# Two-layer attention and MLP block on one core: the first chunk's residual is added from the bf16 input in place, with the list of priorities annealed again

## The chip, the cores and the metric

The kernel runs on one core of a Trainium2 chip. The metric is the device time of one execution in microseconds. Times of before are of five runs; a profiled execution of the same kernel has its own time and its own span (from its first to its last instruction). In the profile PE is TensorE, PEld its weight loads, DVE VectorE, ACT ScalarE, POOL GpSimd and SP SyncE, which here only issues DMAs.

## The reference

The input x has 2048 rows of 576 numbers in bf16. Two layers are applied, each made of an attention block and an MLP block, both with a residual, and with the same weights in both layers:

```python
def _A_ref(x, wqkv, wo):          # H = 32 heads of Dh = 18, window W = 256
    q, k, v = split(x @ wqkv)
    scores = q k^T * Dh**-0.5, masked to 0 <= i - j < W
    return (softmax(scores) v) @ wo

def _B_ref(x, w1, b1, w2, b2):    # F = 4608
    y = _layernorm(x)
    return gelu(y @ w1 + b1) @ w2 + b2

x = x + _A_ref(_layernorm(x), A_wqkv, A_wo)
x = x + _B_ref(_layernorm(x), B_w1, B_b1, B_w2, B_b2)
(the same two lines again)
```

(`split` and the masked line are shortened here; the rest is as it stands.)

## The kernel before

The rows are cut into 16 tiles of 128, four tiles to a chunk, so that there are eight chunks: 0 to 3 of the first layer, 4 to 7 of the second. For each chunk k the kernel does: normalise and project to q, k, v (`qkv`, matmuls on L671, copies by DVE on L710 and L697); attention in eight groups of four heads (`E`: scores on L757, exp by ACT on L766, mask by POOL on L787, product with v on L804, division by the sums on L814 and L819 into `attq`); `tail`: transposes of `attq` to `attT` by DMA (L848), the output projection with `wo` (L671 again), the residual add (`resid`, L838, by DVE), statistics (L592, L594), the reciprocal root (L603, L605, by POOL), the normalised tile (L615, L620) and its transpose by DMA to `xnTm` (L635); and the MLP in two halves of 2304 hidden columns: `G_part` (matmuls on L881 and L893, gelu by ACT on L896 into `hT`) and `mm2` (matmuls on L922, and the residual add through `resid` again).

The residual stream lives in `x_res`, float32, all 16 tiles. Two things share memory with other data. The bf16 input `x_in` lies in the memory of `hT`, which is first written by the gelus of chunk 0; these writes wait for the readers of the input tiles under them (`xin_under`, L898). The q and k of chunk 1 (`qx`, `kx`) lie in the part of `x_res` that belongs to chunks 3 and 2; that is why scores of chunk 1 are shown as `ps<-x_res`. Input tiles get into `x_res` by four DMAs of four tiles each that widen bf16 to float32, issued by POOL (`x_load`, L555 to L558, shown on L536 where all plain DMAs are recorded). For chunk 0:

```python
wo_load()                             # on ACT's queue, after attq of group 0
x_load(0, n0, ["aq1"], -4)            # after attq of group 1
x_load(CH[1][1], CH[1][2], ["aq3"], 0)
w1_load(-1, ["aq3"])
```

SP issues, in one order, the DMA transposes (of q and k on L729, of normalised tiles on L635, of `attq` on L848) and the loads of w1 and w2. ACT issues the loads of wqkv and of wo. SP, ACT and POOL each issue in their instruction order, so a DMA whose wait is not yet met holds all that is behind it.

The order of every engine's instructions is made when the kernel is built. Each operation is entered with the engine, what it reads and writes, a cost, a latency and a priority, and `Plan.schedule` (L257) lays the operations out as a list scheduler: of those that are ready it takes the one that can start first, and of equal ones the one with the smaller priority number; matmul filler goes into the first free of three PSUM banks. `PL.nudge` (L446 to L451) adds a number to the priority of named stages: "q2.1" is the projection of tile 1 of chunk 2, "ea2" and "eb2" the attention of chunk 2, "t2" its tail, "ga2" and "gb2" the halves of its MLP's first matmul, "ma2" and "mb2" of its second, "ld0+" the loads entered with chunk 0. With other numbers the same operations come in another order. Where PE would be idle early in the run, the planner puts in matmuls on a tile of zeros (L579), which nothing reads.

Of the kernel before, what the change touches and what calls it, by code (L numbers as in the profile page):

```python
# [8 lines left out]
ALU = mybir.AluOpType  # L9
# [31 lines left out]
class Sched:  # L41
# [23 lines left out]
    def add(self, eng, fn, reads=(), writes=(), dma=None, ring=4):  # L65
        waits = {}

        def want(ev):
            c, v, _e = ev
            if waits.get(c, 0) < v:  # L70
                waits[c] = v

        for r in reads:
            lw = self.last_write.get(r)
            if lw is not None and not (eng == "pe" and lw[2] == "pe"):
                want(lw)
        for w in writes:
            for rd in self.readers.get(w, ()):
                if rd[2] != eng or rd[3]:
                    want(rd[:3])  # L80
            lw = self.last_write.get(w)
            if lw is not None and not (eng == "pe" and lw[2] == "pe"):
                want(lw)
        if dma is None:
            assert eng != "sp"
            c = self.cnt[eng]
            amount = 1
        else:
            rg = self.ring(eng, dma, ring)
            c = rg.sems[rg.i % rg.k]  # L90
            rg.i += 1
            amount = 16
            if c.val > 0:
                want((c, c.val, None))
        wl = []
        wd = self.waited[eng]
        for cc, v in waits.items():
            if wd.get(cc, 0) >= v:
                continue
            wd[cc] = v  # L100
            wl.append((cc, v))
        c.val += amount
        own = None if dma is not None else eng
        ev = (c, c.val, own)
        self.steps[eng].append(Step(eng, fn, wl, c, amount))
        for w in writes:
            self.last_write[w] = ev
            self.readers[w] = []
        for r in reads:
            self.readers.setdefault(r, []).append((c, c.val, own, dma is not None))  # L110
        return ev
# [297 lines left out]
def build_kernel(nc, A_x, A_wqkv, A_wo, B_x, B_w1, B_b1, B_w2, B_b2, out):  # L409
# [12 lines left out]
    HB = 288  # L422
# [19 lines left out]
    PL = Plan(S, 7)  # L442
    add = PL.add


    PL.nudge = {"b": 1.83, "ea0": -1.98, "ld0+": 40.46, "eb0": 2.23, "q1.0": -6.02, "q1.1": 1.09, "t0": 6.35, "ga0": -26.49, "q2.0": 12.46,  # L446
                "q2.2": 12.06, "q2.3": 21.72, "t1": -35.56, "ea2": -3.78, "ga1": -4.7, "ma1": 15.69, "ma1+": -9.39, "q3.2": -1.65, "q3.3": -7.2,
                "eb3": 1.74, "ma2": 3.52, "q4.0": 39.31, "q4.2": 6.69, "q4.3": -1.19, "t3": 50.91, "mb2": 75.66, "mb2+": -12.34, "eb4": 2.23,
                "ma3": 19.38, "q5.3": 4.22, "t4": -3.2, "ln6": 1.17, "ga4": 2.93, "ma4": 3.37, "q6.0": 2.8, "q6.1": 2.68, "q6.3": 11.39, "t5": 14.34,
                "gb4": 5.24, "ln7": 19.99, "ea6": 18.52, "mb4": 22.88, "ma5": 16.32, "q7.0": 16.24, "q7.1": 29.31, "q7.2": 33.42, "q7.3": 24.98,  # L450
                "t6": 73.06, "gb5": 28.24, "mb5": 74.41, "ga6": -3.51, "eb7": -2.5, "t7": -1.07}  # L451

    def sb(name, shape, dtype):
        return nc.alloc_sbuf_tensor(name, shape, dtype)

    x_res = sb("x_res", [P, NT, D], FP32)
# [29 lines left out]
    def bank(i):  # L486
        if isinstance(i, Bank):
            i = i.no
        return ps[:, i * 512:(i + 1) * 512]
# [12 lines left out]
    x_in = hT[:, :, :].rearrange("p a b -> p (a b)").rearrange("p (t d) -> p t d", d=D)  # L502
# [26 lines left out]
    def dma(q, out_, in_, reads=(), writes=(), cls="w", ring=8, **kw):  # L529
        n = 2 if cls != "xr" else 4  # L530
        for s in out_.shape:
            n *= s
        kw.setdefault("lat", 2.0)
        kw.setdefault("move", n / 330e3)
        kw.setdefault("desc", n // 1152)
        add(q, lambda e: e.dma_start(out_, in_), reads=reads, writes=writes, dma=cls, ring=ring, **kw)  # L536

    n0 = CH[0][2]
# [16 lines left out]
    def x_load(a, cnt, reads, prio):  # L555

        dma("pool", x_res[:, a:a + cnt, :], x_dram[a * P:(a + cnt) * P, :].rearrange("(t p) d -> p t d", p=P), reads=reads,
            writes=[r for t in range(a, a + cnt) for r in X(t)] + {8: ["kx0", "kx1"], 12: [f"qx{i}" for i in range(4)]}.get(a, []), cls="xr", ring=8, cost=1.2, prio=prio)  # L558
# [9 lines left out]
    for i in range(NQN):  # L568
        add("pool", lambda e, i=i: e.memset(qn[:, i, :].rearrange("p (h e) -> p h e", e=32)[:, :, DH:32], 0.0),
            writes=[f"qn{i}h{h}" for h in range(2)], cost=0.5, prio=-9)  # L570
# [260 lines left out]
        for p in pend:  # L831
            pv(k, *p, prio - 0.1)

    def resid(t, hh, b, prio, outp=None):
        src = bank
        sl = slice(hh * HB, (hh + 1) * HB)
        if outp is None:
            add("dve", lambda e: e.tensor_tensor(x_res[:, t, sl], bank(b)[:, 0:HB], x_res[:, t, sl], ALU.add),  # L838
                reads=[b], writes=[f"x{t}h{hh}"], cost=0.375, lat=0.14, prio=prio)
        else:  # L840
            add("dve", lambda e: e.tensor_tensor(xn[:, outp, sl], bank(b)[:, 0:HB], x_res[:, t, sl], ALU.add),
                reads=[b, f"x{t}h{hh}"], writes=[f"xn{outp}" if hh == 0 else f"xd{outp}"], cost=0.375, lat=0.14, prio=prio)

    def tail(k, prio):
        l, t0, nt = CH[k]
        rd = [f"aq{g}" for g in range(G)]
        for i in range(nt):
            add("sp", lambda e, i=i: e.dma_start_transpose(attT[:, :, i * 128:(i + 1) * 128], attq[:, i, :]),  # L848
                reads=rd + ["aqd"], writes=[f"aT{i}"], dma="t", ring=8, cost=1.3, lat=0.6, move=0.72, desc=640, prio=prio - 0.1)
        for i in range(nt):  # L850
            t = t0 + i
            bs = two_out(lambda c, i=i: attT[:, c, i * 128:(i + 1) * 128], lambda c, s: wo_sb[:, c, s:s + HB],
                         [f"aT{i}", "woA", "woB", "woC"], prio)
            for o in range(2):
                resid(t, o, bs[o], prio)
            ln_stats(t, prio)
            ln_rstd([t], True, prio)
            ln_norm_T(t, i, xnTm[:, k % 2], f"xm{k % 2}_", prio, dup=True)
# [82 lines left out]
    def ln1(k, prio):  # L941
        l, t0, nt = CH[k]
        ts = list(range(t0, t0 + nt))
        ln_rstd(ts, False, prio)
        for i, t in enumerate(ts):
            ln_norm_T(t, i, xnTa, "xa", prio)
# [10 lines left out]
    for i in range(n0):  # L957
# [4 lines left out]
        cost=0.5, prio=-1)  # L962
    dma("sp", b2bc[:, :], bass.AP(tensor=B_b2.tensor, offset=B_b2.offset, ap=[[0, P], [1, D]]), reads=["k3"], writes=["b2"], cls="b", ring=2,
        cost=0.5, prio=-1)
    add("pe", lambda e: e.transpose(bank(bb).bitcast(BF16)[:, 0:NF], b1in[:, :], ident[0:NF, 0:NF]), reads=["b1i", "ident"], writes=[bb],
        cost=0.1, lat=0.22, prio=5, alloc=[bb])
# [24 lines left out]
    for k in range(NK + 1):  # L991
        b = 4 * k
        last = k == NK
        if not last:
            if 1 < k < NK - 1:
                PL.stage = f"ln{k + 1}"
                ln1(k + 1, b + 1)
            PL.stage = f"ea{k}"
            E(k, range(0, CUT.get(k, 4)), b - 0.5)
            PL.stage = f"ld{k}"  # L1000
            if k == 0:
                wo_load()
                x_load(0, n0, ["aq1"], -4)
                x_load(CH[1][1], CH[1][2], ["aq3"], 0)
                w1_load(-1, ["aq3"])
        if k >= 2:
            PL.stage = f"mb{k - 2}"
            mm2(k - 2, 1, b)
            w2_load(0, b + 1)
        if k >= 1:  # L1010
            PL.stage = f"ga{k - 1}"
            G_part(k - 1, 0, b + 1)
        if k == 1:
            w2_load(0, 1, True)
        if not last:
            PL.stage = f"eb{k}"
            E(k, range(CUT.get(k, 4), 8), b + 1.5)
            PL.stage = f"le{k}"
            if k == 0:
                w1_load(-1, ["aq6"])  # L1020
            if k == 1:
                for n, kk in enumerate(later):
                    x_load(CH[kk][1], CH[kk][2], [], b + 2)
                    if kk > 2:
                        stats0(kk)
        if k >= 1:
            PL.stage = f"ma{k - 1}"
            mm2(k - 1, 0, b + 2)
            w2_load(1, b + 3)
        if not last:  # L1030
            if k + 1 < NK:
                for i in range(CH[k + 1][2]):
                    PL.stage = f"q{k + 1}.{i}"
                    qkv(k + 1, i, b + 2.2 + 0.2 * i)
            if k == 0:
                PL.stage = f"ln2"
                ln1_in(2, 1)
            PL.stage = f"t{k}"
            tail(k, b + 1.9)
            if k == 0:  # L1040
                w1_load(-1, ["xm0_0"])
        if k >= 1:
            PL.stage = f"gb{k - 1}"
            G_part(k - 1, 1, b + 3)
# [53 lines left out]
```

The softmax here doesn't subtract the row's maximum and nothing guards it: scores larger than these inputs give would overflow.

## Time and profile before

| | us |
|---|---|
| Median of five runs | 929.1 |
| Lowest and highest of the five | 928.2 and 931.24 |
| The profiled execution, its own time | 930.16 |
| Its span | 928.1 |
| PE busy in the span | 899.9 |
| ACT busy | 598.7 |
| POOL busy | 365.3 |
| DVE busy | 317.0 |
| First matmul of the first MLP stage, from the start of the span | 101.94 |

The span begins with the first instruction and ends with the last; the 2.1 us between it and the execution's time lie around it. A matmul is shown from its start to its modelled end, so consecutive matmuls overlap in the record, and PE's work is better taken from one start to the next. The mean granted clock of PE is 0.998 of full speed.

### The profile page before, as it was taken

Reading aid. Unit: us, or ns where it says so; the run is one execution under the profiler, and the core shown is the slowest. Engines: PE = TensorE matmul, PEld = TensorE weight load, DVE = VectorE, ACT = ScalarE, POOL = GpSimd, SP = SyncE. Lnnn points to the kernel's source line nnn. Section 1 sums busy time; section 2 is a strip of 40 time slices with the busy share of each in tenths; the row PEclk is TensorE's granted clock in tenths of the full one; section 3 lists DMA queues with packets and bytes.
Section 4 is the critical chain, followed back from the end, with each engine's and each line's share of the span. In section 5 each row is a group of like instructions: output and inputs, shape, how many; then the busy total and the mean of one; then the engine's idle time right before and its main releaser. Section 6 shows DMA issues by size and latency. Waiting matters only on the chain. (4 is left out here: it accounts for less than half of the span.)

```text
span 928.1 us, 22424 instructions
## 1 busy us (share of the span) xinstructions
PE 899.9 (97%) x9374; PEld 566.6 (61%) x9411; DVE 317.0 (34%) x797; ACT 598.7 (65%) x721; POOL 365.3 (39%) x505
## 2 busy tenths in 40 slices
PE   8989899999999999999999999999999999999998
PEld 6656465565756757477464756656576564657556
DVE  5646311841334403176020723145123430241001
ACT  4877687667836777662777667656685777852541
POOL 3766444462613526161350644315443363610100
PEclk9999999999999999999999999999999999999999
DMA  8797839944196332842739451683618516174430
GB/s 195 137 197 136 190 113 200 218 124 131 34 199 175 117 115 93 192 101 50 227 42 273 73 169 62 166 197 58 202 43 208 156 55 217 32 210 149 154 115 26
DMA packets 204596, 128.85 MB, mean 139 GB/s; under 512 B 128848, under 2 KB 202448, under 8 KB 204496
## 3 DMA queue, kind: packets, MB, share of 16 engines
q1 hardware_dynamic: 199952, 120.06, 52.4%
q0 software_dynamic: 2112, 4.72, 2.2%
q10 hardware_dynamic: 2432, 2.65, 0.9%
q8 instruction: 74, 1.21, 0.5%
q14 instruction: 26, 0.21, 0.1%
HBM read 91.87 MB, written 2.36 MB: 102 GB/s over the span
## 5 line engine op out<-in xcount | busy, mean ns | idle before, releaser
L766 ACT ACTIVATE pT<-ps 128x1024 bf16<-128x1024 f32 (+2 forms) x384 | 348.8, 970 | 123.8 <-PE ps L757 122.0
L787 POOL TENSOR_SCALAR_AFFINE_SELECT pT<-pT 128x512 bf16<-128x512 bf16 (+1 forms) x368 | 281.0, 786 | 273.9 <-ACT pT L766 263.6
L922 PE MATMUL ps<-w_sb,hT 128*128 128x288 bf16 x2304 | 313.6, 286 | 1.5 <-DVE x_res L838 1.5
L896 ACT ACTIVATE hT<-ps,b1col 128x512 bf16<-128x512 f32 x288 | 198.0, 688 | 174.8 <-PE ps L893 172.1
L893 PE MATMUL ps<-xnTm,w_sb 128*128 128x512 bf16 x1115 | 255.0, 379 | 3.0 <-issue 1.7
L922 PEld LDWEIGHTS ps<-w_sb,hT 128*128 128x128 bf16 x2304 | 211.8, 97 | 71.5 <-issue 16.7
L893 PEld LDWEIGHTS ps<-xnTm,w_sb 128*128 128x128 bf16 x1152 | 108.9, 98 | 138.0 <-issue 17.4
L838 DVE TENSOR_TENSOR x_res<-ps,x_res 128x288 f32<-128x288 f32 x160 | 71.2, 450 | 234.6 <-PE ps L922 213.0
L671 PE MATMUL ps<-wqkv,xnTa 128*128 128x288 bf16 x960 | 135.7, 288 | 4.5 <-DVE qn L710 2.9
L804 PEld LDWEIGHTS ps<-vA,pT 128*128 128x128 bf16 x2880 | 94.2, 96 | 27.0 <-POOL pT L787 11.2
L671 PEld LDWEIGHTS ps<-wqkv,xnTa 128*128 128x128 bf16 x960 | 87.3, 98 | 38.2 <-DVE qn L710 7.8
L804 PE MATMUL ps<-vA,pT 128*128 128x20 bf16 x2880 | 100.2, 172 | 5.1 <-POOL pT L787 3.0
L710 DVE CAST qn<-ps 128x288 bf16<-128x288 f32 x120 | 54.1, 454 | 119.5 <-PE ps L671 119.1
L904 POOL TENSOR_TENSOR x_res<-x_res,b2bc 128x576 f32<-128x576 f32 x32 | 40.8, 1276 | 115.5 <-ACT hT L896 115.4
L757 PE MATMUL ps<-qT,kT 32*128 32x384 bf16 (+2 forms) x1216 | 64.1, 276 | 4.0 <-ACT pT L766 3.0
L814 DVE RECIPROCAL rinv<-ps 128x16 f32<-128x16 f32 x64 | 16.2, 253 | 129.1 <-PE ps L804 128.8
L603 POOL TENSOR_SCALAR vtmp<-mv_all 128x1 f32<-128x1 f32 (+1 forms) x43 | 8.8, 204 | 109.6 <-DVE mv_all L594 108.0
L592 DVE BATCH_NORM_STATS2 st_all<-x_res 128x6 f32<-128x288 f32 x104 | 44.8, 447 | 12.3 <-DMA x_res<-in_A_x_dram 10.8
L671 PE MATMUL ps<-wo_sb,attT 128*128 128x288 bf16 x320 | 45.0, 286 | 2.0 <-DMA attT<-attq 1.2
L881 PE MATMUL ps<-xnTm,w_sb 64*128 64x512 bf16 x288 | 39.5, 377 | 2.3 <-DMA xnTm<-xn 1.4
L615 DVE TENSOR_SCALAR xn<-x_res,mv_all,rstd 128x576 bf16<-128x576 f32 x52 | 36.4, 704 | 14.3 <-DMA xnTm<-xn 8.8
L757 PEld LDWEIGHTS ps<-qT,kT 32*128 32x128 bf16 x1216 | 19.5, 92 | 34.5 <-issue 18.6
(43 smaller groups left out, 284.5 us busy)
## 6 DMA issues: line engine op xcount, KB each, us to landing
w_sb<-in_B_w_dram SPq DMA_DIRECT2D x48, 864.0 KB, 6.3
w_sb<-in_B_w_dram SPq DMA_DIRECT2D x48, 768.0 KB, 4.8
w_sb<-in_B_w_dram SPq DMA_DIRECT2D x96, 48.0 KB, 4.4
x_res<-in_A_x_dram POOLq DMA_DIRECT2D x4, 1152.0 KB, 9.9
out_dram<-xn SPq DMA_DIRECT2D x16, 144.0 KB, 1.8
wqkv<-in_A_wqkv_dram ACTq DMA_DIRECT2D x3, 576.0 KB, 7.5
hT<-in_A_x_dram SPq DMA_DIRECT2D x2, 576.0 KB, 5.5
wo_sb<-in_A_wo_dram ACTq DMA_DIRECT2D x1, 576.0 KB, 6.3
```

The source lines that it names most:

```text
L592: add("dve", lambda e, i=i, s=s: e.bn_stats(st_all[:, t, i, :], s[:, t, i * HB:(i + 1) * HB]), reads=res, writes=[f"st{t}_{i}"], cost=0.37 ...
L671: ins = e.matmul(bank(bs[o])[:, 0:HB], lhs(c), rhs(c, o * HB), start=(c == 0), stop=(c == KD - 1))
L710: add("dve", lambda e, b=bs[o], dst=dst: e.tensor_copy(dst, bank(b)[:, 0:HB].rearrange("p (h d) -> p h d", d=DH)), reads=[bs[o]], writes=[ ...
L757: ins = e.matmul(two(bs[j // 2])[:, j % 2, col:col + nq * 128], k_of(T0 + so)[0][32 * j:32 * j + 32, g, :], qs[32 * j:32 * j + 32, g, qo * ...
L766: add("act", lambda e, h2=h2: e.activation(pT[:, sl, 2 * h2:2 * h2 + 2, lo:hi], two(bs[h2])[:, :, lo:hi], ACT.Exp, scale=SCALE), reads=[bs ...
L787: add("pool", lambda e, ap=ap, pat=pat, sgn=sgn, kind=kind: e.affine_select(ap, ap, pattern=pat, compare_op=(ALU.is_ge if kind == "d" else ...
L804: ins = e.matmul(bank(B_O)[:, o:o + VW], pT[:, sl, j, col + qi * 128:col + (qi + 1) * 128], vA[:, (T0 + so) % VS, 4 * g + j, :], start=(fi ...
L838: add("dve", lambda e: e.tensor_tensor(x_res[:, t, sl], bank(b)[:, 0:HB], x_res[:, t, sl], ALU.add), reads=[b], writes=[f"x{t}h{hh}"], cos ...
L893: ins = e.matmul(bank(bk)[:, 0:n], w1_sb[:, sl, col:col + 128], xnTm[:, k % 2, c, 0:n], start=False, stop=(c == 3))
L896: add("act", lambda e, ff=ff, fl=fl, bk=bk: e.activation(hT[:, fl, 0:n], bank(bk)[:, 0:n], ACT.Gelu_apprx_tanh, bias=b1col[:, ff:ff + 1]), ...
L904: add("pool", lambda e, t=t: e.tensor_tensor(x_res[:, t, :], x_res[:, t, :], b2bc[:, :], ALU.add), reads=["b2", f"h{fl}"], writes=X(t), co ...
L922: ins = e.matmul(bank(b)[:, 0:HB], hT[:, fl, i * 128:(i + 1) * 128], w2_sb[:, fl, hh * HB:(hh + 1) * HB], start=(fl == 0), stop=(fl == NFH ...
```

## The change

The residual add of the first attention block's first chunk (tiles 0 to 3) takes its second operand from the bf16 input tile `x_in`, in the memory of `hT`, and writes the sum to `x_res` in float32, where it added to the float32 copy in `x_res` before. The `x_load` of these four tiles is taken out; those of the other twelve tiles stay. The table of priorities is another one, found by annealing anew for the changed program. Of the table only its beginning is shown; every entry differs or is new.

```diff
-    PL.nudge = {"b": 1.83, "ea0": -1.98, "ld0+": 40.46, "eb0": 2.23, "q1.0": -6.02, "q1.1": 1.09, "t0": 6.35, "ga0": -26.49, "q2.0": 12.46,
...
+    PL.nudge = {"b": 25.97, "eb0": 10.41, "q1.0": -51.04, "q1.1": 4.1, "q1.2": 3.12, "q1.3": 3.03, "t0": 20.85, "ga0": -7.27, "q2.0": 7.44,
...
-    def resid(t, hh, b, prio, outp=None):
+    def resid(t, hh, b, prio, outp=None, first=False):
         src = bank
         sl = slice(hh * HB, (hh + 1) * HB)
-        if outp is None:
+        if first:
+            add("dve", lambda e: e.tensor_tensor(x_res[:, t, sl], bank(b)[:, 0:HB], x_in[:, t, sl], ALU.add),
+                reads=[b, f"xin{t}"], writes=[f"x{t}h{hh}"], cost=0.375, lat=0.14, prio=prio)
+        elif outp is None:
...
             for o in range(2):
-                resid(t, o, bs[o], prio)
+                resid(t, o, bs[o], prio, first=(k == 0))
...
                 wo_load()
-                x_load(0, n0, ["aq1"], -4)
                 x_load(CH[1][1], CH[1][2], ["aq3"], 0)
                 w1_load(-1, ["aq3"])
```

Built, the changed program has these differences in its instructions: one DMA fewer on POOL's queue; two warming matmuls fewer (44 instead of 46); the eight adds named above read `hT` instead of `x_res`; everything else is the same set of instructions in another order. PE's order is unchanged up to about 27 us of the profile of before and in its last 120 rows (runs of equal instructions).

## The prediction, made before the changed kernel was run

> **What bounds the kernel now.** I read the page first (busy shares, the groups that the change touches, the DMA issues), then the timeline of PE up to the first MLP stage, then the timelines of SP and POOL and the windows over the same stretch. From the page:
>
> ```profile
> PE 899.9 (97%) x9374; PEld 566.6 (61%) x9411; DVE 317.0 (34%) x797; ACT 598.7 (65%) x721; POOL 365.3 (39%) x505
> ...
> L838 DVE TENSOR_TENSOR x_res<-ps,x_res 128x288 f32<-128x288 f32 x160 | 71.2, 450 | 234.6 <-PE ps L922 213.0
> ...
> x_res<-in_A_x_dram POOLq DMA_DIRECT2D x4, 1152.0 KB, 9.9
> ```
>
> PE is busy 97% of the span, so only its stalls are to be had: 28.2 us without any matmul. The gaps of at least 0.15 us in PE's timeline add up to 20.4 us; 11.0 us of these lie before 103 us, where the first chunks' attention runs, and the other 9.4 us are spread over the following 822 us. Two places before 103 us matter here. The first is the handover from the attention of chunk 0 to that of chunk 1 (timeline of PE; columns start, duration, instruction, in brackets the idle time ahead of it and what ended it):
>
> ```profile
> 64.89 0.25 PE L804 MATMUL ps<-vA,pT 128*128 128x20 bf16 x4
> 66.54 0.35 PE L804 MATMUL ps<-vA,pT 128*128 128x20 bf16 x8 [1.41 <-issue]
> 67.73 1.38 PE L671 MATMUL ps<-wqkv,xnTa 128*128 128x288 bf16 x5 [0.83 <-DMA xnTa<-xn]
> 69.04 0.51 PE L757 MATMUL ps<-x_res 32*128 32x384 bf16 x4
> 69.59 1.38 PE L671 MATMUL ps<-wqkv,xnTa 128*128 128x288 bf16 x5
> ```
>
> Five matmuls that take 0.79 us elsewhere take 1.38 us here: after the idle time the granted clock is half. The second place is the end of chunk 0's output projection:
>
> ```profile
> 90.49 0.56 PE L804 MATMUL ps<-vA,pT 128*128 128x20 bf16 x16 [1.15 <-POOL pT L787]
> ...
> 97.84 0.40 PE L757 MATMUL ps<-x_res,kT 32*128 32x256 bf16 x8 [1.13 <-ACT pT L766]
> ...
> 101.94 0.82 PE L881 MATMUL ps<-xnTm,w_sb 64*128 64x512 bf16 x6 [1.36 <-DMA xnTm<-xn]
> ```
>
> What makes the handover late is seen on the two queues that issue DMAs. POOL issues the float32 copies of chunk 0 (41.51) and of chunk 1 (48.16); SP, which issues in order, then needs 5 and 7 us for a transpose that takes it 1.2 us elsewhere:
>
> ```profile
> 41.51 0.97 POOL L536 DMA_DIRECT2D x_res<-in_A_x_dram  x1
> 48.16 0.78 POOL L536 DMA_DIRECT2D x_res<-in_A_x_dram  x1
> ```
> ```profile
> 50.53 5.06 SPq L729 DMA_TRANSPOSE x_res<-qn  x1
> 55.69 7.07 SPq L729 DMA_TRANSPOSE kT<-qn  x1
> 62.85 1.32 SPq L635 DMA_TRANSPOSE xnTa<-xn  x1
> ```
>
> The windows (length, busy time of PE, PEld, DVE, ACT, POOL, clock, DMA share, GB/s) show the 16 DMA engines overfull from 46 to 70 us, with little moved from 52 to 58 us:
>
> ```profile
> 46.00:52.00 6.00, 5.49 (x86) 3.69 (x85) 2.91 (x8) 5.24 (x8) 4.41 (x7) 1.00 1.21 283
> 52.00:58.00 6.00, 5.39 (x94) 3.44 (x90) 2.91 (x7) 4.46 (x7) 3.51 (x5) 1.00 1.35 124
> 58.00:64.00 6.00, 5.72 (x92) 3.59 (x85) 2.37 (x6) 5.46 (x8) 4.73 (x7) 1.00 1.52 215
> 64.00:70.00 6.00, 3.75 (x37) 1.96 (x37) 1.62 (x5) 2.14 (x4) 2.28 (x3) 0.80 1.14 178
> ```
>
> **What the Trainium skill says.** "DMA: Bandwidth & Descriptors", section "Issuing engines are not separate DMA queues": DMAs from any engine run on the same 16 DMA engines and interleave. The trace agrees: SP's transposes stretch while POOL's load moves. "VectorE: DVE Perf Modes", section "The perf-mode tier table": a tensor_tensor with an operand in PSUM stays at the single rate, so a bf16 second operand should not shorten the add; the trace has the add only with a float32 one (450 ns) and can't confirm it. "TensorE: Matmul & The Clock Gate", Part 1: an idle window of about 3.4 us halves PE's clock; here the trace has clock 0.5 from 67.7 to 71.1 us after 2.2 us of idle in two pieces. "Advanced Engine Details and Errata", section "ISA Cache": instructions come in lines of 16 KB. The page's instruction queue has 74 packets of 1.21 MB, 16 KB each, and one falls into 64 to 66 us; that the 1.41 us before which PE "waited for nothing shown" is such a fetch held up by full DMA engines is my inference.
>
> **The change part by part.**
>
> Removed: one load of 1.18 MB as written. Its issue held POOL 0.97 us; POOL was busy 5.81 of 6.00 us in 40 to 46, but no PE stall named POOL there: 0. Its bytes held the DMA engines from about 43.6 to 48.1 us. Behind it stood wo (issued 43.33 and 43.73, landed 49.6 and 51.4, needed at 76.12: 0) and the transpose issued at 44.66 (landed 51.64 instead of some 3 us after its issue). ACT's second wo issue took 1.55 us against 0.37 for the first, and the exp behind it started 0.59 us late. ACT's 48 exps of chunk 0 take 8 x (1.94 + 1.51 + 1.08) = 36.2 of the 45 us from 20.8 to 65.8, so ACT is close to the bound there: 0.5 us gained.
>
> The adds: 8 of the 160 at L838 read bf16. From nothing to 0.3 us shorter or longer each way in all; I take 0. The removed wait was for a load that landed at 48.1 us, and the first add ran at 76.93: 0. The first gelus now wait for these adds as well, since the input lies under hT; each add comes before the normalisation that feeds the same MLP stage, so it is long done: 0.
>
> The new order moves nearly everything on PE between 27 us and the last chunk's tail; its last 120 rows are unchanged. I priced both orders with start-to-start distances from PE's timeline (122 ns for 288 columns, 216 ns for 512, 25 ns for an attention-value matmul, 0.2 to 0.3 us for a group of row-tiled scores with its change of tiling). They give 863.9 us before and 863.5 us after (two warming matmuls fewer): 0.4 gained. What is left is where stalls go.
>
> Handover. PE's last value matmuls would end at 65.2 and, after one five-matmul group, scores of chunk 1 would start at 65.8; they start at 69.04, 3.2 us late, and half clock until 71.1 costs another 1.0. Of these 4.2 us I expect 3.0 back: DMA work worth 4.5 us is gone ahead of the critical transposes, and chunk 1's load is issued after 20 mask instructions instead of 22, some 1.2 us earlier. The rest stays, because chunk 1's load still meets transposes and a w1 load. Lower end 0, upper end 4.2. Next late is then ACT's exp chain.
>
> Between the first score of chunk 1 and the first MLP stage the new order has 26.5 us of priced PE work instead of 25.6. If ACT sets the handover this costs 0.9, if PE sets it nothing: 0.5 lost.
>
> Tail of chunk 0. From the last wo matmul to the first MLP matmul the priced distance grows from 8.3 to 9.8 us; POOL's rstd pairs stand one by one between masks instead of two in a row (86.66 to 88.5, ahead of the 1.15 us stall); the fourth tile's normalisation has 3 DVE instructions after its statistics instead of 7. But SP now has three q/k transposes among the four of attT. Of 1.15 + 1.13 + 1.36 = 3.6 us I take half: 1.8 gained, ends -1 (lost) and 3.6.
>
> After 103 us the stalls of 9.4 us are dealt anew. One is likely to go: 1.19 us at 262.26, where wo follows the last value matmul by 4.2 us of priced work; the new order's smallest such distance is 5.0. Others can come. I take 0, ends 3 either way.
>
> Sum: 0.5 + 0.4 + 3.0 - 0.5 + 1.8 = 5.2 us. The profiled execution took 930.16 us with a span of 928.1, so 925.0; the five runs' median is 929.1, 1.1 lower, and 929.1 - 5.2 is about 924.0.
>
> **The rivals.** Stalls stay (same): the removed load had landed at 48.1, while the slow stretch is 53 to 63 us, when chunk 1's load and transposes share the engines, and that pair is still there. Then only 0.4 + 0.5 + about 0.4 of the tail come back, less 0.5: 928.3. For it speaks the 124 GB/s of 52 to 58 us; against it that everything in that stretch had been pushed back by 3 to 4 us.
>
> All of it goes (faster still): 4.2 + 3.6 + 0.9 and 1.3 from later stages: 919. It needs an early landing of every transpose.
>
> SP's queue becomes the bound (slower): the three q/k transposes among the attT ones each wait for a copy by DVE, and everything behind them on SP waits too: attT, then wo, adds, normalisation, xnTm and the whole first MLP stage. Before, the fourth attT landed at 81.06 and was used at 87.5, 6.4 us to spare; three more issues at 1.27 take 3.8 and the earlier place of wo 1.1, which leaves 1.5 us. If each of the three waits 2.3 us, as the slowest one did at 77.60, 6.9 - 1.5 = 5.4 us pass on to the first MLP stage, 2.4 us more than the handover gives: with 0.5 us for the longer stretch 932. It decides from a fourth attT that lands more than about 16 us after chunk 0's last value matmul.
>
> **How the numbers follow.** About 0.2% (1.9 us) is what a measurement of this kernel tells from no change. Forecast 0.48 (924.0, its own range 921 to 927); still faster 0.14 (919); stalls stay 0.15 (928.3, of which 0.03 beyond 0.2% faster); slower 0.23 (932, SP's queue or a worse deal of later stalls, half of it above). Faster 0.65, same 0.12, slower 0.23. Leaving out half of the slow case above 932 and less than half of the fastest below 919 leaves some 0.17 out: 919 to 932.
>
> **What would show it.** Right: no half clock after the first 10 us, SP issues near 1.3 us between 50 and 63 us, the first score of chunk 1 near 66 us, first MLP matmul at about 97 us instead of 101.94, and later stages shifted by the same amount. Wrong: 5 us issues on SP still there, a gap before wo's matmuls on attT, or an early gain that is lost between 103 us and the last chunk.

## The result and the profile after

| | before | changed |
|---|---|---|
| Median, runs side by side on the same chips | 928.2 us (75 runs, 923.8 to 932.6) | 931.84 us (40 runs, 929.3 to 935.1) |
| Ratio to before, 95% interval | | 1.0039 [1.003, 1.0048] |
| The profiled execution and its span | 930.16, 928.1 | 930.79, 929.0 |

The changed kernel is about 0.4% slower; the forecast was 5.2 us, some 0.55%, faster. The two profiled executions lie only 0.6 us apart because that of before was 2 us above its median and that of after 1 us below. This turned out to be the main point: the forecast took from the profile of before a stall that this one execution had and that a second profile of the same kernel does not have.

The page of the profile after, with the lines that answer to those of before. PE has three matmuls fewer in the record and 0.6 us less busy time, eight adds have left the float32 group, and three loads of 1152 KB remain:

```profile
PE 899.3 (97%) x9371; PEld 564.4 (61%) x9409; DVE 321.9 (35%) x797; ACT 598.4 (64%) x721; POOL 364.6 (39%) x504
...
L841 DVE TENSOR_TENSOR x_res<-ps,x_res 128x288 f32<-128x288 f32 x152 | 68.0, 450 | 225.3 <-PE ps L925 198.8
...
x_res<-in_A_x_dram POOLq DMA_DIRECT2D x3, 1152.0 KB, 8.5
```

The handover from chunk 0 to chunk 1 in PE's timeline after (start, duration, instruction, in brackets the idle time ahead and what ended it). The first scores of chunk 1 (`ps<-x_res`) start at 65.80 us after a wait of 0.16, and ten projection matmuls take 1.40 us: full clock. Taken alone this looks like the forecast come true; whether the change did it is a question for the runs.

```profile
65.19 0.45 PE L804 MATMUL ps<-vA,pT 128*128 128x20 bf16 x12
65.80 0.34 PE L757 MATMUL ps<-x_res 32*128 32x384 bf16 x4 [0.16 <-ACT pT L766]
65.96 0.24 PE L757 MATMUL ps<-x_res,kT 32*128 32x128 bf16 x4
66.13 1.40 PE L671 MATMUL ps<-wqkv,xnTa 128*128 128x288 bf16 x10
```

SP's queue in that stretch after. The issues are shorter than the 5.06 and 7.07 us of before, but not back at 1.3 us: the load of chunk 1 is still there, and transposes still wait beside it.

```profile
50.41 1.23 SPq L729 DMA_TRANSPOSE x_res<-qn  x1
53.26 3.69 SPq L729 DMA_TRANSPOSE kT<-qn  x1
57.04 3.92 SPq L729 DMA_TRANSPOSE x_res<-qn  x2
62.11 1.20 SPq L635 DMA_TRANSPOSE xnTa<-xn  x1
```

The windows of after (length, busy us of PE, PEld, DVE, ACT, POOL, then clock, DMA share, GB/s): the trough of 124 GB/s at 52 to 58 us is gone, and from 64 to 70 us PE is busy 5.49 us at clock 1.00, where it was 3.75 at 0.80.

```profile
52.00:58.00 6.00, 5.33 (x92) 3.50 (x88) 2.45 (x6) 5.67 (x8) 4.80 (x8) 1.00 1.33 333
...
64.00:70.00 6.00, 5.49 (x85) 3.60 (x82) 3.60 (x10) 5.16 (x8) 4.19 (x6) 1.00 0.86 157
```

New waits stand elsewhere (PE's timeline after, longest ones). At 30.88 PE comes too early for a transposed tile. At 88.48 it waits 1.85 us for DVE (the division of the group before, which reads the output bank, ended at 88.33, and the statistics that the profile names at 88.45), and the five matmuls at 90.14 then take 1.38 us, half clock. At 376.35 it waits 1.64 us for exps. The first MLP matmul stands at 99.49 us; the forecast had about 97:

```profile
30.88 1.39 PE L671 MATMUL ps<-wqkv,xnTa 128*128 128x288 bf16 x10 [1.25 <-DMA xnTa<-xn]
...
88.48 0.55 PE L804 MATMUL ps<-vA,pT 128*128 128x20 bf16 x16 [1.85 <-DVE mv_all L594]
88.88 0.78 PE L671 MATMUL ps<-wqkv,xnTa 128*128 128x288 bf16 x5
89.60 0.61 PE L757 MATMUL ps<-x_res,kT 32*128 32x256 bf16 x8
90.14 1.38 PE L671 MATMUL ps<-wqkv,xnTa 128*128 128x288 bf16 x5
...
99.49 0.82 PE L884 MATMUL ps<-xnTm,w_sb 64*128 64x512 bf16 x6
...
376.35 0.82 PE L884 MATMUL ps<-xnTm,w_sb 64*128 64x512 bf16 x6 [1.64 <-ACT pT L766]
```

So the question for the runs: the stall that was to go has gone, and still the kernel is slower. Either the stall was worth nothing to begin with, or the new order costs more than it gave, or the bf16 adds cost something.

### The profile page after: what moved, and what is told of

It is laid out like the page before. It is cut to its first block, busy times and chain, and to the rows that moved or that the text cites. A ratio compares the mean times of both kernels' runs of the same rounds, so it can differ in the third digit from the quotient of the medians.

```text
span 929.0 us, 22396 instructions
## 1 busy us (share of the span) xinstructions
PE 899.3 (97%) x9371; PEld 564.4 (61%) x9409; DVE 321.9 (35%) x797; ACT 598.4 (64%) x721; POOL 364.6 (39%) x504
## 4 chain that ended last, share of the span: by engine, by line
PE 81%; DMA 4%; POOL 4%; issue 4%; DVE 4%; ACT 2%; SPq 0%; POOLq 0%; DVEq 0%
PE ps L925 27%; PE ps L896 26%; PE ps L671 12%; PE ps L804 7%; PE ps L757 5%; PE ps L884 4%; POOL pT L787 3%; DMA attT<-attq 2%; ACT pT L766 2%; DMA hT<-in_A_x_dram 1%; DMA xnTa<-xn 1%; DVE xn L615 1%; DVE st_all L592 1%; DVE x_res L841 1%; POOL rstd L605 1%
## 5 line engine op out<-in xcount | busy, mean ns | idle before, releaser
L841 DVE TENSOR_TENSOR x_res<-ps,x_res 128x288 f32<-128x288 f32 x152 | 68.0, 450 | 225.3 <-PE ps L925 198.8
L697 DVE CAST vA<-ps 128x288 bf16<-128x288 f32 x64 | 28.9, 455 | 56.9 <-PE ps L671 56.5
```

## The experiments

Three theories stood at the start. A: dropping the load gains what was forecast, and the new order loses more later. B: the stall at the handover was an accident of one execution, the load is worth nothing, and only the order costs. C: the bf16 adds, or the longer life of the input, cost time. "Before" in each group of four runs is the kernel before on the same chip: 926.38 us (27 runs), 927.26 (27) and 927.54 (46).

### First group: taking the change apart

**Data without order (e1).** The load is planned but not issued, so every other instruction keeps the place it had before.

```diff
         for st, t in order:
+            if t.fn is None:
+                continue
...
                 x_load(0, n0, ["aq1"], -4)
+                PL.tasks[-1].fn = None
```

(with the changed `resid` of the changed kernel.)

> The instructions of before in exactly the order of before; only chunk 0's float32 load is left out and its eight adds read the bf16 input. Theory A (the load's removal gains, the new order loses more later): faster than before by 0.2 to 0.5%, about 925 us where before has 928.2. Theory B (the handover stall of the profile was a chance of that one execution, the load is worth nothing, the new order alone costs): within 0.1% of before. Theory C (the adds from bf16 or the input's longer life cost time): slower than before by 0.2% or more.

Measured: 925.83 us, ratio 0.9991 [0.9979, 1.0002].

**Tables exchanged (e2, e3).** The program of before with the new table, and the changed program with the old table; in both, the planner lays out its own order from them. The tables are the two of the change; e2 puts back the load and the float32 adds, e3 takes them out.

> The program of before, with the load and the float32 adds, planned with the new table of priorities. Theories A and B: slower than before, by 0.4 to 0.8% (the whole loss is in the order that the table makes). Theory C: within 0.1% of before.

Measured: 938.61 us, ratio 1.0132 [1.0107, 1.0157].

> The change without its new table: load left out, adds from bf16, planned with the table of before. The planner still moves things, since POOL has one task fewer. Theory A: faster than before by 0.1 to 0.5% if the planner keeps the later order, theory B: within 0.2% of before, theory C: slower by 0.2% or more.

Measured: 937.92 us, ratio 1.0123 [1.0099, 1.0147]. PE's longest wait in each of the two profiles is for exps ahead of an MLP group of six matmuls: 2.31 us at 150 us in e2, 2.13 at 153 in e3.

**Order without the removal (e4).** The changed kernel in its exact order, with the load of chunk 0 issued again by POOL behind fifteen masks; the adds go on reading bf16, so nothing needs what it loads.

```diff
+            if self.extra_fn is not None and t.eng == "pool" and t.dma is None and seen and masks >= 15:
+                self.S.add("pool", self.extra_fn, ["aq1"], self.extra_writes, dma="xr", ring=8)
...
+    PL.extra_fn = lambda e: e.dma_start(x_res[:, 0:4, :], x_dram[0:4 * P, :].rearrange("(t p) d -> p t d", p=P))
```

> The changed program in exactly its order, with chunk 0's load put back on POOL's queue where before had it (after 15 masks); what it loads is overwritten by the adds. Theory A: slower than the changed kernel by 0.2 to 0.5%, so 0.6 to 0.9% slower than before. Theory B: the same as the changed kernel, 0.3 to 0.5% slower than before. Theory C: the same as the changed kernel.

Measured: 934.53 us, ratio 1.0083 [1.0062, 1.0104]. The changed kernel has 1.0039 in the result above, and 1.006 [1.004, 1.008] in the next group (e6), with which this interval overlaps.

What follows: e1 leaves of A at most 0.2%, well short of the forecast, and with the bf16 adds in it and no loss it rules out C in the order of before. e3 by itself came out as C had it, and e2 lost more than A and B had expected; but e1 has the same adds as e3 without a loss, so what e3 loses lies in the order that the planner made. Either table with the other program costs 1.2 to 1.3%: these two tables are each a setting for the program that they were annealed for. e4 looked as if the load cost some 0.4% in the new order; e12 comes back to that.

### Second group: does the stall recur, and what do the new waits cost?

**Before once more (e5), after once more (e6)**, unchanged, for second profiles and for a ratio of before to itself.

> The kernel before, unchanged. Theory 'chance' (the 4.2 us stall and half clock at the handover of the profiled execution of before were an accident of that one execution): this profile has no clock of 0.5 between 60 and 75 us and at most 1 us of idle PE there, its span is near 924, and the ratio to before is 1.000 within 0.1%. Theory 'standing stall' (the float32 load causes it every time): 2 to 4 us of idle and half clock at 65 to 71 us again, span near 928.

Measured: 926.45 us, ratio 0.9988 [0.9972, 1.0004]; span 924.6. The ratio is a hair outside the 0.1% expected, with 1 inside its interval.

> The changed kernel, unchanged. Theory 'new order costs': ratio 1.003 to 1.005 to before; PE's gaps of 1.2 us at about 31, 1.8 us at about 88 and 1.6 us at about 376 are there again in this second profile. Theory 'accident': the ratio falls to within 0.1% of 1, and at least two of these three gaps are gone.

Measured: 932.65 us, ratio 1.006 [1.004, 1.008]; span 930.7. This is a little above the 1.003 to 1.005 expected.

The handover in the second profile of before, with the load in place. The scores of chunk 1 start at 65.69 us; there is no stall and no half clock:

```profile
64.38 0.45 PE L804 MATMUL ps<-vA,pT 128*128 128x20 bf16 x12
64.99 0.77 PE L671 MATMUL ps<-wqkv,xnTa 128*128 128x288 bf16 x5 [0.16 <-ACT pT L766]
65.69 0.34 PE L757 MATMUL ps<-x_res 32*128 32x384 bf16 x4
...
66.02 0.79 PE L671 MATMUL ps<-wqkv,xnTa 128*128 128x288 bf16 x5
```

And SP's queue in the same execution. The first long issue is there again, the second is 4 us shorter than in the first profile, and the transpose of `xnTa` behind them is issued at 57.80 us, where it was 62.85:

```profile
50.02 4.60 SPq L729 DMA_TRANSPOSE x_res<-qn  x1
54.71 2.99 SPq L729 DMA_TRANSPOSE kT<-qn  x1
57.80 1.23 SPq L635 DMA_TRANSPOSE xnTa<-xn  x1
```

What else differs is the load of chunk 1, which the change leaves in. The list of DMA issues gives its time from issue to landing, in the first profile of before (issued at 48.16 us) and then in e5 (issued at 47.25):

```profile
x_res<-in_A_x_dram POOLq DMA_DIRECT2D x1, 1152.0 KB, 15.9
x_res<-in_A_x_dram POOLq DMA_DIRECT2D x1, 1152.0 KB, 10.0
```

So it landed at 64.0 us in the first profile and at 57.3 in e5; in after, e1, e9 and e6 it took 8.5 to 11.0 us. The load of chunk 0, the one that the change removes, took 6.6 and 6.5 us in the two executions of before and had landed ahead of all this.

That agrees with B: the stall is absent with the load of chunk 0 in place (e5) and in e1 without it (first scores at 65.38). How often before has the stall is open; if removing the load removed it, the interval of e1 allows no more than 2 us of gain on average. e6 has the waits of the changed kernel again: 1.11 us at 30.93, 1.85 at 88.52, 1.64 at 376.24.

**One move (e7).** The last scores of chunk 3's attention go ahead of ten projection matmuls, so that the exps that the MLP group waits for start earlier. Tasks are named by their number in the plan; 1588 are the scores, 1658 the projection half before them.

```diff
+        for who, behind in [(1588, 1658)]:
+            m = next(x for x in order if x[1].idx == who)
+            order.remove(m)
+            order.insert(next(i for i, x in enumerate(order) if x[1].idx == behind) + 1, m)
```

> The changed kernel with one move on PE: the last scores of chunk 3 go ahead of ten projection matmuls, so that their exps end about 1.2 us earlier and free the banks for the six-bank MLP group. If the 1.64 us gap at 376 us is lost for good: the gap shrinks to about 0.4 and the time falls by 1.2 us, ratio to the changed kernel 0.9987. Rival (it only hides another wait): the gap moves to another place within 10 us and the time falls by less than 0.4 us.

Measured: 931.25 us, ratio 1.0046 [1.0031, 1.0062], against 1.006 for e6 on the same chip: 1.4 us less in the medians, though the intervals overlap. PE's timeline at the place, in the first profile of before (no wait) and in e6. Scores come first, then values, then the MLP group:

```profile
371.11 0.40 PE L757 MATMUL ps<-qT,kT 32*128 32x256 bf16 x8
371.44 2.01 PE L671 MATMUL ps<-wqkv,xnTa 128*128 128x288 bf16 x15
373.28 0.55 PE L804 MATMUL ps<-vA,pT 128*128 128x20 bf16 x16
373.76 0.82 PE L881 MATMUL ps<-xnTm,w_sb 64*128 64x512 bf16 x6
```
```profile
373.71 0.40 PE L757 MATMUL ps<-qT,kT 32*128 32x256 bf16 x8
374.04 0.56 PE L804 MATMUL ps<-vA,pT 128*128 128x20 bf16 x16
376.24 1.19 PE L884 MATMUL ps<-xnTm,w_sb 64*128 64x512 bf16 x6 [1.64 <-ACT pT L766]
```

and of e7, where the ten projections stand between them and 0.42 us of the wait is left:

```profile
375.46 0.40 PE L761 MATMUL ps<-qT,kT 32*128 32x256 bf16 x8
375.79 1.40 PE L675 MATMUL ps<-wqkv,xnTa 128*128 128x288 bf16 x10
377.03 0.55 PE L808 MATMUL ps<-vA,pT 128*128 128x20 bf16 x16
377.99 0.82 PE L888 MATMUL ps<-xnTm,w_sb 64*128 64x512 bf16 x6 [0.42 <-ACT pT L770]
```

**Three moves (e8).** The one of e7, and two in the front: at 31 us a projection half (306) and its copy (308) go behind the next scores (166); at 86 us the reciprocal and the division (487, 488) go ahead of a tile's normalisation on DVE.

```diff
+        for who, behind in [(1588, 1658), (306, 166), (308, 306), (487, 417), (488, 487)]:
```

> The changed kernel with the move of the run with one move and two more: the first projection half of chunk 1 that waits for its transposed tile at 31 us goes behind the scores that were next (removes up to 1.2 us), and at 86 us the reciprocal and the division go ahead of the normalisation of a tile on DVE (removes 0.5 us, after which the masks at 87.9 bind). If the named gaps are the cost of the new order: 1.2 + 1.2 + 0.5 = 2.9 us less than the changed kernel, about 1.001 of before. Rival (the front is held by ACT's exp chain and transposes, so front gaps come back at the next wait): only 1.2 to 1.6 us less, about 1.0025 of before.

Measured: 931.25 us, ratio 1.0047 [1.0032, 1.0062]: as e7. The rival holds for the front: 1.4 us less than e6, as e7 alone gives. At 31 us 0.55 us of wait for a copy by DVE is left, of 1.11 in e6. Instead of the 1.85 us wait, e8 has these two, for masks of POOL and for DVE's residual add:

```profile
87.59 0.56 PE L808 MATMUL ps<-vA,pT 128*128 128x20 bf16 x16 [1.14 <-POOL pT L791]
88.56 0.66 PE L675 MATMUL ps<-wqkv,xnTa 128*128 128x288 bf16 x4 [0.41 <-DVE x_res L842]
```

### Third group: the steady part, and the load again

**e1 once more (e9)**, the same program on another chip.

> The load left out and the eight adds reading bf16, in exactly the order of before; the same program as in the first group of runs, on another chip. If the data part of the change is worth nothing: ratio to before 0.998 to 1.000, as it was (0.9991). If it is worth the 5 us of the forecast: 0.9945.

Measured: 926.07 us, ratio 0.9991 [0.9978, 1.0004], the same figure as in the first group.

**e1 with two moves (e10).** Six MLP matmuls (1161) go ahead of the output projection at 258 us; a normalisation (2720) and its transpose (2721) go behind two copies at 633 us.

```diff
+        for who, behind in [(1161, 1160), (2720, 3018), (2721, 2720)]:
```

> The program of the run before this one with two moves: at 258 us one group of six MLP matmuls goes ahead of the first output-projection matmuls, which wait 0.9 us for their transpose, and at 633 us two copies go ahead of a normalisation on DVE that waits for a DMA, which holds up a projection by 1.0 to 1.2 us. If stalls of the steady part cost their length: 1.9 us less than the run before this one, ratio to before about 0.997. Rival (a later wait takes their place): less than 0.8 us.

Measured: 925.21 us, ratio 0.9979 [0.9969, 0.999]; 0.9 us below e9, half of what its first theory expected. It is the only version here whose interval against before lies wholly below 1; the intervals of e9 and e10 overlap, so what the two moves are worth is not resolved by the times. In the traces both waits go: that at 633 us, 0.97 us in e9, is absent in e10. The wait for the transposed tile in e9:

```profile
256.03 2.37 PE L927 MATMUL ps<-w_sb,hT 128*128 128x288 bf16 x18
259.38 1.40 PE L673 MATMUL ps<-wo_sb,attT 128*128 128x288 bf16 x10 [0.99 <-DMA attT<-attq]
```

and in e10, where six more matmuls cover it but for 0.22 us:

```profile
254.79 3.10 PE L934 MATMUL ps<-w_sb,hT 128*128 128x288 bf16 x24
258.11 2.08 PE L680 MATMUL ps<-wo_sb,attT 128*128 128x288 bf16 x14 [0.22 <-DMA attT<-attq]
```

**The changed kernel with moves in the steady part (e11).** The one of e7, and three between 279 and 307 us: an MLP group ahead of the output projection, a value group behind an MLP group, and the value projections of two tiles exchanged with their copies.

```diff
+        for who, behind in [(1588, 1658), (1419, 1418), (1352, 1428)]:
...
+        for one, other in [(1685, 1643), (1686, 1644), (1687, 1645), (1688, 1646)]:
+            i, j = (next(n for n, x in enumerate(order) if x[1].idx == w) for w in (one, other))
+            order[i], order[j] = order[j], order[i]
```

> The changed kernel with the move at 376 us and three more in the stretch from 279 to 307 us, where the new order puts output projection, attention values and projections close behind their transposes and masks (waits of 0.34, 0.44 and 0.88 us). If the steady waits are the cost of the new order: 1.3 + 1.6 = 2.9 us less than the changed kernel, and 0.5 us more where the half clock after the 376 us wait goes too; ratio to before about 1.002. Rival (they only move on): like the run with one move, about 1.0046.

Measured: 929.97 us, ratio 1.003 [1.0019, 1.004]. Against 1.0039 and 1.006 for the changed kernel this is between the two expectations. Of the three waits at 279 to 307 us two moved on, to a transposed q and to the masks of a later group (PE's timeline of e11):

```profile
287.39 0.40 PE L764 MATMUL ps<-qT,kT 32*128 32x384 bf16 x8 [0.68 <-DMA qT<-qn]
...
295.50 0.56 PE L811 MATMUL ps<-vA,pT 128*128 128x20 bf16 x16 [0.56 <-POOL pT L794]
```

**e11 with the load put back (e12)**, in the way of e4.

> The run before this one with the float32 load of chunk 0 put back on POOL behind fifteen masks; the adds still read bf16. If the load costs something in the new order (as the first such run seemed to show): 3 to 4 us more than the run before this one. If it is free wherever its issue is covered, as in the order of before: within 0.8 us of it.

Measured: 931.31 us, ratio 1.005 [1.0031, 1.0069]: 1.3 us above e11, between the expectations, with intervals that overlap. The 0.4% that e4 seemed to show for the load in the new order is not confirmed, and a smaller cost is not excluded.

### Where the new order loses

The traces of six executions can be laid against one scale. I took the priced PE work of the prediction as the scale (each matmul at its start-to-start distance) and noted how far the start of each matmul lags behind it. The growth of that lag in us:

| Priced PE work | order of before: e5, e1, e9 | new order: after, e6 | e11 |
|---|---|---|---|
| 0 to 100 | 17.6, 17.1, 17.4 | 19.1, 19.2 | 19.3 |
| 100 to 256 | 10.6, 10.2, 12.0 | 9.5, 9.0 | 9.3 |
| 256 to 300 | 2.7, 2.7, 2.7 | 4.9, 5.1 | 4.3 |
| 300 to 336 | 2.1, 2.1, 2.1 | 2.0, 2.0 | 2.0 |
| 336 to 344 | 0.3, 0.3, 0.3 | 2.2, 3.8 | 1.0 |
| 344 to 480 | 5.1, 4.5, 4.5 | 6.5, 6.6 | 6.8 |
| 480 to the end | 18.9, 18.8, 18.8 | 18.1, 18.2 | 18.0 |

The means of after and e6 and of the three others differ by 6.1 us, more than the medians (3.6), so the table shows where time goes rather than how much in a usual execution. The first profile of before, laid against the same kind of scale, grows by 3.8 us more than e5 up to 100 and stays within 0.3 us of it over all the rest together: the stall of the handover again. Between after and e6 and the other three the front is nearly a wash: 1.8 us lost up to 100, 1.7 won back up to 256. This balance is no firmer than the spread of single executions: e7 has the order of e6 up to the move at 376 us, and its MLP group there starts at 377.99 instead of 376.24 although it waits 1.2 us less, so it had lost some 3 us more on the way. What remains is lost in three places of the steady part: 2.3 us at 256 to 300 (about 285 to 335 us of the trace), 2.7 at 336 to 344 (the wait at 376), 1.8 at 344 to 480; 0.7 comes back later. e11 won back 2.0 of the second and 0.7 of the first. The third was not tested by a move.

## Why the prediction was wrong, step by step

**The handover, 3.0 us of 4.2: the step that failed.** The late transposes read from the profile were there in that execution, and the stall is absent in the changed kernel as foretold. But it is absent in e5 as well, which is the kernel before with its load. So the step that tied the stall to the removed load failed, and the gain was booked from one execution; e1 and e9, which remove the load and nothing else, both give 0.9991, and before against itself gives 0.9988. The warning was in the numbers: the profiled execution took 930.16 us and the median was 929.1, and 4 us in one place is more than that difference. The rival "stalls stay" had the right argument, that the load had landed at 48.1 us and the pair that slows the transposes from 53 us on is still there; only the stall itself did not stay. In that execution chunk 1's load took 15.9 us to land instead of 8.5 to 11.0, the second transpose beside it took 7.07 us to issue, and the transpose that ends PE's wait of 0.83 us was issued 5 us later than in e5. What slowed the load in that one execution stays open, and so does the wait of 1.41 us ahead. For that one the prediction suspected a fetch of 16 KB of instructions, with "Advanced Engine Details and Errata", "ISA Cache": one began at 64.04 us and took 1.15 us. In e5 one began at 65.35, took 1.73 us, and PE did not wait, so a fetch alone does not do it.

**Stalls after 103 us "dealt anew, 0": the second step that failed.** From priced 100 (some 120 us of the traces) on the table gives -1.7 + 2.3 + 2.7 + 1.8 - 0.7, with -0.1 at 300 to 336, together 4.3 us lost in after and e6. That is beyond the ends of 3 us given for it. A zero for a complete reordering took better and worse distances as equally likely. But in the order of before most of the waits in the steady part were already covered: its lag grows by 2.7 and 0.3 us at 256 to 300 and 336 to 344, so there was little to win and much to lose. e7 and e11 show by removal that at least the wait at 376 us (1.64 us, of which 1.2 go) belongs to the order. For the rest of the loss the table says where it is, not why; and why the annealing chose an order with these waits was not looked into. One step of the working could have found it: the prediction priced the distance from value matmuls to wo throughout, but not the distance from the last scores of an attention half to the MLP group that needs six banks. There the new order has one value group of 0.4 us, where the old one has fifteen projection matmuls more and no wait.

**The tail of chunk 0, 1.8 gained, and the longer stretch, 0.5 lost: wrong.** The first MLP matmul stands at 99.49 and 99.62 us in the changed kernel, against 98.16, 97.61 and 97.99 in e5, e1 and e9. So it is some 1.6 us later than in a usual execution of the old order, not 1.3 earlier. Of the three stalls named, the ones for masks (1.15) and for exps (1.13) recur in e5, e1 and e9 within 0.02 us, and the last one with 1.1 to 1.6; of the three the new order has only 0.41 us for exps, but 1.85 us at 88 us in their place. e8 shows what stands behind that wait: with DVE's normalisation out of its way, 1.14 us for POOL's masks remain. In after and e6 this loss is won back by 256; in e7 it is not.

**The wo issue, 0.5, and the priced work, 0.4.** In e5 the exp behind the second issue starts 0.20 us late with the load, against 0.59 in the first profile; e1 has no such delay, and shows at most 2 us of gain from everything together. 0.5 was again the figure of one execution. The priced work can't be told apart from the spread.

**The adds, 0: right.** The eight with a bf16 operand take 430 ns on average against 450. This agrees with "VectorE: DVE Perf Modes", "The perf-mode tier table", which gives a tensor_tensor with an operand in PSUM the single rate whatever the other operand is.

**SP's queue becomes the bound: did not happen.** The fourth attT was issued at 79.24 us and needed at most 4.5 us to land, so at most 14.5 us after chunk 0's last value matmul (69.2), below the 16 from which this rival decided; no wo matmul of chunk 0 waits for a transpose. That the kernel ended where this rival's price lay, near 932, is chance: the mechanism was another.

## What to carry to other kernels

Before a stall of one profiled execution is booked as a gain, ask whether the median can contain it: compare that execution with the median, and look for the stall in a second profile. A change that comes with a new order of everything is two changes; measure its data part in the exact old order, and price the new order's distances at every kind of wait (transposes, masks, banks for the next group), not only at the place that the change is about. Removing a wait often uncovers the next one, in the front (e8) and in the steady part (two of three in e11); of the 1.7 us of steady waits that are gone in e10's trace, 0.9 us showed in the median.

## What the runs showed of the hardware that was not expected

**Half clock after less than an idle window.** "TensorE: Matmul & The Clock Gate", Part 1, puts the half clock after at least one idle window of about 3.4 us. Each stretch at clock 0.5 between 60 and 900 us lasts 3.41 us in the clock record, which agrees with its window; but in none of the traces was what went before a whole idle window; the most was 2.19 us of idle PE (e2, 151.71). In the 3.41 us ahead of the drop PE was idle for 2.18 us (before, 67.66), 1.85 (after, 89.51; e6, 89.85; e11, 89.17), 1.80 (e7, 90.84), 1.64 (e6, 376.57; e4, 378.35) and 1.56 (e8, 89.25). Here the measurement decides: about half that length can be enough. It is not always enough. After has the 1.64 us at 376 us without the drop, e4 the 1.85 us ahead of 88.53, and in e12 that wait is followed by five matmuls at 0.77 us, full clock:

```profile
90.31 0.55 PE L820 MATMUL ps<-vA,pT 128*128 128x20 bf16 x16 [1.85 <-DVE mv_all L610]
90.71 0.77 PE L687 MATMUL ps<-wqkv,xnTa 128*128 128x288 bf16 x5
91.41 0.40 PE L773 MATMUL ps<-x_res,kT 32*128 32x256 bf16 x8
91.74 0.79 PE L687 MATMUL ps<-wqkv,xnTa 128*128 128x288 bf16 x5
```

The page calls the window free-running; where it falls against the wait may decide, which no run here tests. The price can be read at 376 us: after and e6 both have the 1.64 us wait there, only e6 the half clock, and from 336 to 344 of priced work it loses 1.6 us more.

**Spread.** Executions of one unchanged kernel on one chip went from 923.5 to 932.6 us (27 runs), about 1%, nearly twice the effect that was forecast. The same load of chunk 1 took 15.9 us to land in the first profile of before, and 8.0 to 11.0 us in the thirteen others.
